# The wq gradient of seven head groups stored in five blocks each instead of one or three pieces

## The chip, the cores and the metric

The kernel runs on one core of a Trainium2 chip. The metric is the device time of one execution in microseconds (us), lower is better. Engines are named as in the profile: PE is TensorE (matmul, with its weight loads PEld), DVE is VectorE, ACT is ScalarE, POOL is GpSimd and SP is SyncE. Transfers between the device memory and the on-chip memory are issued from SP, ACT or POOL and are carried out by the core's 16 DMA engines.

## What is computed

The reference is one decode step (one token, model width 640) of a block with two parallel branches, together with the gradients of everything but the second branch's own input:

```python
xn  = layernorm(x)                                  # 1 x 640
A   = attention(xn; 32 heads of 128, K and V caches of 8192 rows each) @ wo
B   = (silu(xn @ w1) * (xn @ w3)) @ w2              # F = 1728
out = x + A + B
_out, _vjp = jax.vjp(_f, A_x, A_k_cache, A_v_cache, A_wq, A_wo, B_w1, B_w3, B_w2)
_grads = _vjp(grad_out)                             # a gradient as large as each input
```

All arrays are bf16. The two caches have 64 MB each (in units of 2^20 bytes), and so have their gradients; each is read or written once. `wq` is 640 x 4096 and its gradient `out_4` has the same shape: it is the outer product of `xn` (640 values) with the gradient of the query row (4096 values), so column block g of it belongs to the four heads of group g.

## The kernel before

**Staging.** The heads are handled one after another, h = 0 to 31. For each head one tile of K and one of V (128 partitions x 16 KB, 2 MB) is loaded into one of ten slots, transposed on PE in pieces, used for the scores, and then overwritten in place on DVE by the gradient of the same shape (`outer`, L464), which is stored from the same slot. `fifo` (L104) issues all of these on SP; SP works through its list in order. `store` (L477) issues the store of a slot and then, through `load_next` (L122), the next load into a slot that has become free, so the load waits until the slot's earlier store has landed.

**Groups.** Four heads make a group, eight groups in all (`NG`). A group has a tile `wq_g` (128 partitions x 5 blocks x 512 columns, 640 KB; block ci holds the input rows 128 ci to 128 ci + 127, one row a partition, 1 KB each) and a tile `wo_g` (640 KB). Three buffers of each kind rotate (`wpool`). `load_group` (L109) loads them, from group 3 on through POOL's queue, when the group three before is finished.

**The gradients of a group** are made one group later, spread over the next group's heads by `side_k`, `side_m` and `side_v` (L684 to L715): at its head 0 `fin_od`, `fin_pe` and `fin_wo` (the wo gradient, stored by `store_group`), at its head 1 the blocks 0, 1 and 2 of the wq gradient, at its head 2 the blocks 3 and 4. `fin_wq(g, ci)` (L524) makes one block with two DVE instructions: L527 multiplies the block by the query gradient and sums it for the input's gradient, L529 writes the block of the wq gradient over it. In the trace the five blocks of group 1 are ready at 233.5, 235.9, 240.4, 250.7 and 253.1 us. After block 4 the whole tile is stored and the loads of group g + 3 are issued behind it on POOL; these write the same buffers, so they wait for the store's landing.

**How the tile is stored.** `store_group` (L505) knows three ways. Groups 0 and 6: one POOL transfer of the whole tile (L512). Groups 1 to 5, called with `split`: partitions 0 to 4 and 5 to 125 as two POOL transfers (L508), partitions 126 and 127 through `fifo` on SP (L509, shown as L105). Group 7, at the end of the kernel: partitions 0 to 67 on SP (L514), 68 to 72 and 73 to 127 on POOL (L516). The wo gradient goes the first way for groups 0 to 6 and the third way for group 7.

**The end.** After the last head the gradients of group 7 are made all at once (L836 to L840), then the two small rows `out_0` and `out_1` are stored from SP.

**The second branch** (`mlp`, L557) runs once, ahead of head 2, and its weight gradients leave from POOL.

Of the kernel before, what the change touches and what calls it, by code (L numbers as in the profile page):

```python
# [16 lines left out]
P = 128  # L17
# [4 lines left out]
def kernel(  # L22
# [22 lines left out]
    nc = tc.nc  # L45
# [9 lines left out]
    NG = H // GH  # L55
    GW = GH * DH
# [23 lines left out]
    dwq_v = out_4.rearrange("(ci p) n -> p ci n", p=P)  # L80
# [23 lines left out]
    def fifo(out_, in_):  # L104
        nc.sync.dma_start(out_, in_)  # L105
# [3 lines left out]
    def load_group(g, eng):  # L109
        wq_g = wpool.tile([P, NC, GW], BF16, name="wq_g", tag="wq_g")  # L110
        eng.dma_start(wq_g[:], wq_v[:, :, g * GW:(g + 1) * GW])
        wo_g = wpool.tile([P, GH, D], BF16, name="wo_g", tag="wo_g")
        eng.dma_start(wo_g[:], wo_v[:, g * GH:(g + 1) * GH, :])
        grp[g] = dict(wq=wq_g, wo=wo_g)
# [387 lines left out]
        for hh in range(GH):  # L502
            out_row(G_["od_bf"][:, hh, 0:1], G_["wo"][:, hh, :])

    def store_group(g, dst, t, split=False):  # L505
        if split:
            for lo, hi in ((0, 5), (5, 126)):
                nc.gpsimd.dma_start(dst[lo:hi], t[lo:hi])  # L508
            fifo(dst[126:P], t[126:P])  # L509
            return  # L510
        if g < NG - 1:
            nc.gpsimd.dma_start(dst, t[:])  # L512
            return
        fifo(dst[0:68], t[0:68])  # L514
        for lo, hi in ((68, 73), (73, P)):
            nc.gpsimd.dma_start(dst[lo:hi], t[lo:hi])  # L516

    def fin_wo(g):
        G_ = grp[g]
        for hh in range(GH):  # L520
            nc.vector.tensor_scalar(G_["wo"][:, hh, :], g_bc[:], G_["od"][:, hh, 0:1], None, ALU.mult)
        store_group(g, dwo_v[:, g * GH:(g + 1) * GH, :], G_["wo"])

    def fin_wq(g, ci):  # L524
        G_ = grp[g]
        wq_g, dqb = G_["wq"], G_["dqb"]
        nc.vector.scalar_tensor_tensor(wq_g[:, ci, :], wq_g[:, ci, :], 1.0, dqb, ALU.mult, ALU.mult,  # L527
                                       accum_out=dxa[:, ci, g:g + 1])
        nc.vector.tensor_scalar(wq_g[:, ci, :], dqb, xn_col[:, ci:ci + 1], None, ALU.mult)  # L529
        if ci == NC - 1:  # L530
            store_group(g, dwq_v[:, :, g * GW:(g + 1) * GW], wq_g, 1 <= g <= 5)
            grp.pop(g)
            if g + 3 < NG:
                load_group(g + 3, nc.gpsimd)
# [149 lines left out]
    def side_k(h):  # L684
        g, hh = divmod(h, GH)
        if hh == 1 and g > 0:
            fin_wq(g - 1, 0)
        elif hh == 2 and g > 0:
            fin_wq(g - 1, 3)
        elif hh == 3 and g + 1 < NG:  # L690
            prep_do(g + 1, 1)

    def side_m(h):
        g, hh = divmod(h, GH)
        if hh == 0 and g > 0:
            fin_od(g - 1)
        elif hh == 1 and g > 0:
            fin_wq(g - 1, 1)
        elif hh == 2 and g > 0:
            fin_wq(g - 1, 4)  # L700
        elif hh == 3 and g + 1 < NG:
            prep_do(g + 1, 2)
            prep_do(g + 1, 3)
# [195 lines left out]
```

## Time and profile before

| | before |
|---|---|
| time, median of 3 runs | 728.27 us (727.76, 728.27, 730.0) |
| the profiled execution: its span | 728.3 us (the profile gives no other time for it) |
| bytes moved | 303.53 MB, mean 417 GB/s |
| busy share of the span: PE, DVE, ACT, POOL | 82%, 63%, 52%, 5% |
| packet time of SP's queue (q1), of POOL's (q0), as a share of 16 DMA engines | 90.4%, 8.8% |
| mean granted TensorE clock | 0.927 of full speed |

The page gives, for 40 equal slices of the span, how busy each engine and the DMA engines were; a digit is tenths. "q1 hardware_dynamic" is the queue that SP issues on and "q0 software_dynamic" the one that POOL issues on; a queue's share is the time that its packets took, out of 16 engines' span. A line of DMA issues names the tiles (destination, source), the issuing engine, how often, the size and the median time from issue to landing. In a table by stage each engine has its busy time and, in brackets, its number of instructions, followed by the granted clock, the DMA share and GB/s. The trace also holds each DMA packet (start, duration, size, queue; not which of the 16 engines took it) and, for each transfer, the times at which its semaphore rose: 16 increments where all 16 engines took part.

### The profile page before, as it was taken

How to read it: one execution, taken by the hardware profiler on the slowest of the kernel's cores; microseconds unless marked ns; L12 is line 12 of the kernel's file. 1: busy time of each engine (PE TensorE's matmuls, PEld its weight loads, DVE VectorE, ACT ScalarE, POOL GpSimd, SP SyncE). 2: the span in 40 equal slices, each digit the busy share in tenths (PEclk: the TensorE clock that was granted, in tenths of full speed). 3: DMA queues.
4: the chain of work that ended last, by engine and by line, in shares of the span. 5: the costliest groups of instructions: out<-in, count | busy, mean ns of one | idle time of the engine just before them, and what ended most of it. 6: DMA issues, size and time to landing. Idle time of an engine off the chain costs nothing.

```text
span 728.3 us, 12951 instructions
## 1 busy us (share of the span) xinstructions
PE 600.8 (82%) x5193; PEld 375.6 (52%) x5193; DVE 460.1 (63%) x811; ACT 375.7 (52%) x727; POOL 35.0 (5%) x52
## 2 busy tenths in 40 slices
PE   3989589999999999877986889878896987988840
PEld 2547456665566556544554555445563555644520
DVE  4169646677767886767556746556755665677482
ACT  3640736665666656544554546455562555645410
POOL 0010110000100000000010000000000000000000
PEclk9996799999999999999999989999998999999975
DMA  9999999999999999999999999999999999999996
GB/s 347 398 409 424 427 428 428 413 427 425 418 409 429 427 426 424 423 429 422 425 425 427 431 420 427 421 427 432 410 428 424 428 425 422 429 424 430 429 415 239
DMA packets 28358, 303.53 MB, mean 417 GB/s; under 512 B 3481, under 2 KB 5532, under 8 KB 11658
## 3 DMA queue, kind: packets, MB, share of 16 engines
q1 hardware_dynamic: 22022, 277.14, 90.4%
q0 software_dynamic: 6272, 25.56, 8.8%
q8 instruction: 41, 0.67, 0.4%
q14 instruction: 19, 0.16, 0.1%
q10 hardware_dynamic: 4, 0.00, 0.0%
HBM read 151.34 MB, written 151.34 MB: 416 GB/s over the span
## 4 chain that ended last, share of the span: by engine, by line
DMA 57%; PE 33%; DVE 5%; ACT 2%; issue 1%; SPq 0%; ACTq 0%; DVEq 0%
DMA out_dram<-kv 30%; DMA kv<-in_A_k_cache_dram 18%; PE pT L318 15%; DMA kv<-in_A_v_cache_dram 7%; PE sA L339 4%; PE X L433 3%; PE dA L339 3%; DVE kv L466 2%; PE m L356 2%; DMA wo_g<-in_A_wo_dram 2%; ACT KT L320 1%; PE gu_ps L562 1%; PE dh_ps L573 1%; DVE side L257 0%; PE pT L266 0%
## 5 line engine op out<-in xcount | busy, mean ns | idle before, releaser
L320 ACT COPY KT<-pT 128x512 f32<-128x512 f32 x512 | 287.7, 587 | 230.9 <-PE pT L318 210.3
L318 PE MATMUL pT<-ident_f,kv 128*128 128x128 f32 x2048 | 306.6, 289 | 61.6 <-DMA kv<-in_A_k_cache_dram 29.9
L318 PEld LDWEIGHTS pT<-ident_f,kv 128*128 128x128 f32 x2048 | 236.2, 148 | 155.1 <-issue 59.6
L466 DVE TENSOR_TENSOR kv<-qd,U 128x4096 bf16<-128x4096 bf16 x64 | 146.0, 2283 | 0.0
L466 DVE TENSOR_TENSOR kv<-qd,P 128x4096 bf16<-128x4096 bf16 x64 | 143.5, 2283 | 0.0
L433 PE MATMUL X<-kv,Z 128*32 128x512 bf16 x1024 | 93.5, 402 | 1.8 <-DVE Z L450 1.8
L339 PE MATMUL sA<-KT,qz 128*32 128x512 bf16 x512 | 83.9, 408 | 0.0
L339 PE MATMUL dA<-KT,qz 128*32 128x512 bf16 x512 | 83.3, 404 | 0.0
L416 DVE SCALAR_TENSOR_TENSOR U<-m,P 128x64 bf16<-128x64 f32 x32 | 7.5, 234 | 83.0 <-PE m L356 83.0
L382 DVE TENSOR_REDUCE mrow<-m 128x1 f32<-128x64 f32 x32 | 7.2, 223 | 75.1 <-PE m L356 75.0
L339 PEld LDWEIGHTS <-qz 128*32 128x32 bf16 x1024 | 29.6, 95 | 40.4 <-issue 37.7
L433 PEld LDWEIGHTS <-Z 128*32 128x32 bf16 x1024 | 32.4, 99 | 33.8 <-issue 5.7
L356 PE MATMUL m<-selc,KT 64*128 64x64 f32 x256 | 30.7, 243 | 8.6 <-ACT KT L346 8.6
L356 PEld LDWEIGHTS m<-selc,KT 64*128 64x128 f32 x256 | 21.7, 145 | 30.4 <-ACT KT L346 21.6
L376 ACT CAST qd<-pT 128x256 bf16<-128x256 f32 x32 | 11.9, 372 | 40.3 <-DVE kv L466 28.8
L389 DVE TENSOR_REDUCE negM<-m 128x1 f32<-128x128 f32 x32 | 9.3, 291 | 33.2 <-PE m L386 33.2
L527 DVE SCALAR_TENSOR_TENSOR wq_g<-wq_g,side 128x512 bf16<-128x512 bf16 x40 | 27.3, 682 | 0.0
L257 DVE SCALAR_TENSOR_TENSOR side<-wo_g,g_bc 128x640 bf16<-128x640 bf16 x32 | 26.2, 819 | 1.4 <-DMA wo_g<-in_A_wo_dram 1.1
L448 DVE SCALAR_TENSOR_TENSOR U<-m,P 128x128 bf16<-128x128 f32 x32 | 11.4, 355 | 15.8 <-PE m L446 15.8
L406 DVE RECIPROCAL rZ<-m 128x1 f32<-128x1 f32 x32 | 5.3, 166 | 24.2 <-PE m L400 24.2
L346 ACT COPY KT<-dA 64x512 f32<-64x512 f32 x32 | 18.6, 583 | 2.6 <-PE dA L339 2.6
L346 ACT COPY KT<-sA 64x512 f32<-64x512 f32 x32 | 18.6, 580 | 2.3 <-PE sA L339 2.1
(164 smaller groups left out, 377.4 us busy)
## 6 DMA issues: line engine op xcount, KB each, us to landing
out_dram<-kv SPq DMA_DIRECT2D x64, 2048.0 KB, 30.9
kv<-in_A_k_cache_dram SPq DMA_DIRECT2D x32, 2048.0 KB, 27.9
kv<-in_A_v_cache_dram SPq DMA_DIRECT2D x32, 2048.0 KB, 26.0
wq_g<-in_A_wq_dram POOLq DMA_DIRECT2D x7, 640.0 KB, 13.5
wo_g<-in_A_wo_dram POOLq DMA_DIRECT2D x7, 640.0 KB, 19.6
out_dram<-wo_g POOLq DMA_DIRECT2D x7, 640.0 KB, 15.6
kv<-in_B_w_dram SPq DMA_DIRECT2D x2, 1728.0 KB
out_dram<-kv POOLq DMA_DIRECT2D x2, 1728.0 KB, 23.2
```

The costliest lines, as they stand in the source:

```text
L257: nc.vector.scalar_tensor_tensor(junk[:], G_["wo"][:, hh, :], 1.0, g_bc[:], ALU.mult, ALU.mult, accum_out=G_["do"][:, hh:hh + 1])
L318: nc.tensor.transpose(pT[:, k * P:(k + 1) * P], W3[:, 4 * c + k, :], ident_f[:])
L320: nc.scalar.copy(KT[:].rearrange("p k w -> p (k w)"), pT[:])
L339: nc.tensor.matmul(S_[kind][q:q + QW, :], lhsT=S_["qz"][:, o:o + QW], rhs=KTb[c][:, par, :], start=(c0 == 0 and par == 0), stop=(c0 == NCH ...
L346: nc.scalar.copy(XS[0:QH].rearrange("p k w -> p (k w)"), S_.pop(kind)[0:QH, :])
L356: nc.tensor.matmul(S_["m"][:, b0:b0 + 4 * J].rearrange("p (x c k t) -> p k x c t", x=4, k=4, t=2)[:, k], lhsT=XS[0:QH, k, :], rhs=selc[0:Q ...
L376: nc.scalar.copy(qd[:].rearrange("p a d -> p (a d)"), hd[h].pop("ps_r"))
L389: nc.vector.tensor_reduce(S_["negM"][:], S_["m"][:, 2 * J:2 * J + P], AX.X, ALU.max, negate=True)
L433: nc.tensor.matmul(xg["X"][q:q + QW, :], lhsT=Z[:, o:o + QW], rhs=W[:, N4 * i:N4 * (i + 1)], start=(slot == 0 and i < 4), stop=(slot == NS ...
L448: nc.vector.scalar_tensor_tensor(S_["U2"][:], S_["V"][:, 0:J].unsqueeze(2).to_broadcast([P, J, 2]), S_["m"][:, OC + NS:OC + NS + 1], S_["P ...
L466: nc.vector.tensor_tensor(dst[:, lo * DH:hi * DH].rearrange("p (j a b) -> p j a b", a=DH // 2, b=2), vec.rearrange("p (a b) -> p a b", b=2 ...
L527: nc.vector.scalar_tensor_tensor(wq_g[:, ci, :], wq_g[:, ci, :], 1.0, dqb, ALU.mult, ALU.mult, accum_out=dxa[:, ci, g:g + 1])
```

## The change

For groups 0 to 6 each block of the wq gradient is sent from POOL directly behind the DVE instruction that makes it: five transfers of 128 partitions x 1 KB (128 KB) a group, each waiting for its own block. The whole-tile transfer of groups 0 and 6 and the three pieces of groups 1 to 5 are gone, the two partitions on SP among them. Group 7 and all wo gradients are stored as before. The loads of group g + 3 still stand on POOL's queue behind the last block.

```diff
-    def store_group(g, dst, t, split=False):
-        if split:
-            for lo, hi in ((0, 5), (5, 126)):
-                nc.gpsimd.dma_start(dst[lo:hi], t[lo:hi])
-            fifo(dst[126:P], t[126:P])
-            return
+    def store_group(g, dst, t):
         if g < NG - 1:
             nc.gpsimd.dma_start(dst, t[:])
             return
...
         nc.vector.tensor_scalar(wq_g[:, ci, :], dqb, xn_col[:, ci:ci + 1], None, ALU.mult)
+        dwq_g = dwq_v[:, :, g * GW:(g + 1) * GW]
+        if g < NG - 1:
+            nc.gpsimd.dma_start(dwq_g[:, ci, :], wq_g[:, ci, :])
         if ci == NC - 1:
-            store_group(g, dwq_v[:, :, g * GW:(g + 1) * GW], wq_g, 1 <= g <= 5)
+            if g == NG - 1:
+                store_group(g, dwq_g, wq_g)
             grp.pop(g)
             if g + 3 < NG:
                 load_group(g + 3, nc.gpsimd)
```

## The prediction

> **What bounds the kernel now.** I read the page's DMA lines first, then the list of DMA issues, the waits of GpSimd's and SyncE's queues, the busy time by stage at the end, and last the trace's own packet records (start, duration, size and queue of each DMA packet) and the landing increments of each transfer, which the page only sums.
>
> The page: the strip of DMA shares over the span, the bytes moved, and the queues.
>
> ```profile
> DMA  9999999999999999999999999999999999999996
> GB/s 347 398 409 424 427 428 428 413 427 425 418 409 429 427 426 424 423 429 422 425 425 427 431 420 427 421 427 432 410 428 424 428 425 422 429 424 430 429 415 239
> ...
> q1 hardware_dynamic: 22022, 277.14, 90.4%
> q0 software_dynamic: 6272, 25.56, 8.8%
> ```
>
> Every slice but the last is full, and the queues' packet times add up to 99.7% of what 16 engines have (90.4 + 8.8 + 0.4 + 0.1). So the time is the packet time per DMA engine plus the unevenness between engines at the end. PE (82%) and DVE (63%) wait for loads, not the other way round. GpSimd's transfers are q0, SyncE's q1.
>
> The list of DMA issues, the wq gradient's rows: how often, size, median us to landing.
>
> ```profile
> out_dram<-wq_g POOLq DMA_DIRECT2D x5, 605.0 KB, 17.0
> out_dram<-wq_g POOLq DMA_DIRECT2D x2, 640.0 KB, 13.1
> out_dram<-wq_g POOLq DMA_DIRECT2D x6, 25.0 KB, 6.7
> out_dram<-wq_g SPq DMA_DIRECT2D x5, 10.0 KB
> out_dram<-wq_g SPq DMA_DIRECT2D x1, 340.0 KB
> ```
>
> In groups 1 to 5 the tile leaves as 5, 121 and 2 partitions; in groups 0 and 6 whole. The packet records show how these spread. q0 has 55 packets of 3072 B, a size that only a share of 55 rows of 1 KB leaves (13 packets of 4 KB and one of 3 KB): five transfers on eleven engines each, 11 partitions an engine. The five partitions go to the five other engines, one each: a packet of 4 KB and one of 1 KB. A whole tile would give each engine 40 KB. So five times over, eleven engines carry 15 KB more than an even share and five carry 35 KB less.
>
> They are the same five each time. The 16 landing increments of one kv transfer lie within 2.0 us for the load issued at 5.8 us, while for the store issued at 533.0 us the first engine lands 12.9 us before the median and the last 7.5 after it. Of the last kv store (issued at 706.1), five increments come at 712.9 to 713.4 and eleven at 715.0 to 727.4; 727.4 is the last landing of all, and the span ends 0.9 us later. The first 1280 B packets of the last group's 68-partition wo piece start at 712.7 to 713.0, just as the early engines finish: that piece and the 68-partition wq piece run on four of the five. The wq piece lands on those four at 721.7, 722.5, 723.3 and 724.8.
>
> The busy time by stage (us in the stage, busy time and count of each engine, then granted clock, DMA share, GB/s):
>
> ```profile
> 690.00:695.00 5.00, 5.00 (x50) 2.86 (x47) 2.37 (x5) 3.22 (x8) 0.00 (x0) 1.00 0.97 413
> 695.00:700.00 5.00, 3.25 (x37) 1.89 (x31) 4.29 (x7) 0.93 (x2) 0.00 (x0) 1.00 0.98 419
> 700.00:705.00 5.00, 0.17 (x2) 0.08 (x1) 5.00 (x3) 0.17 (x1) 0.00 (x0) 0.50 0.93 393
> ...
> 720.00:725.00 5.00, 0.00 (x0) 0.00 (x0) 0.00 (x0) 0.00 (x0) 0.00 (x0) 0.50 0.44 153
> 725.00:728.30 3.30, 0.00 (x0) 0.00 (x0) 0.00 (x0) 0.00 (x0) 0.00 (x0) 0.50 0.04 15
> ```
>
> Before 705 us some engines already idle: (0.03 + 0.02 + 0.07) x 5 us x 16 = 9.6 us, 1.9 for each of five leaders that run out of issued stores. At the end the reverse: 0.44, then 0.04, a single engine finishing.
>
> **The change, part by part.** Durations are of the one profiled execution, whose span is 728.3 us; that is 0.03 us from the median of 728.27, so the sum needs no correction.
>
> Packet work in total. A whole tile is 160 packets of 4 KB at a median of 159 ns: 25.4 us of engine time, 1.59 per engine. The three pieces are 148 x 159 + 11 x 121 + 5 x 46 + 10 x 46 ns (SyncE's ten packets of 1 KB): 25.6 us. A block of 128 rows gives each of 16 engines 8 rows of 1 KB, two packets of 4 KB, so five blocks are again 160 packets. The nearest row, the 160 KB w2 store of 128 rows, shows such pairing: 32 packets of 5120 B. Transfers of groups 0 to 6: 35 on GpSimd instead of 12 there and 5 on SyncE, 18 more in all. Each GpSimd transfer adds one 4 B packet of 9 ns on each engine: 23 x 9 ns is 0.2 us; against that go the 81 small packets (12 and 16 B, some 10 ns) that each odd-shaped pair shows. Between -0.1 and +0.3 us; I take 0.
>
> GpSimd's issues. Five issues per group for two of 0.6 and 1.06 us; the nearest rows of 128 partitions take 0.56 to 0.88 us, so some 2 us more per group on an engine busy 5% of the span. The cover is that idle time; if it were gone, the next group's loads would start late. Each issue now also waits for its own block on DVE, and behind it in GpSimd's order stand the other blocks and the loads of group g+3. Those loads wait for the stores to land:
>
> ```profile
> POOL out_dram L508 <- DVE wq_g L529: 180.5, 5, 39.9
> POOL wq_g L111 <- DMA out_dram<-wq_g: 111.1, 4, 35.6
> ```
>
> 27.8 us each, since SyncE's two partitions lie behind kv transfers. With five GpSimd blocks the last should land in 6.7 to 13 us, and the loads start some 15 us sooner. Nobody waits: group 4's loads go out from 283.1 and their first reader on DVE comes at 332.6. Bytes moved earlier on a full engine gain nothing: 0.
>
> SyncE loses five issues of about 0.3 us and waits of 0.9 us in all for L529, beside 453 us of waiting for stores: 0.
>
> The balance is what is left. Per group, each of the five engines gets 10 packets for one and a rest: 10 x 159 - (159 + 46) = 1.39 us more, 6.9 over five groups; the two that also carried SyncE's partitions save 5 x 46 ns a group, so 5.8. Each of the eleven drops 3 x 159 + 121 = 0.60 us, 3.0 in all.
>
> The eleven: their last kv landing moves from 727.4 to 724.4.
>
> The four with the 68-partition pieces: kv done at 713.0, of which 1.9 us was idle that now disappears, so 711.2 (rounded), + 6.9 = 718.1. Then the two pieces. Before, from 713.0 to a mean landing of 723.1 is 10.1 us, the last of the four 1.7 later; from the packets at their medians it is 68 x 55 + 85 x 46 ns, 7.6 us. Below is excluded by the count of packets; above, many of the 1280 B packets took 90 to 250 ns with the other engines still at work. I take 10.1, since those engines will be at work again: 718.1 + 10.1 + 1.7 = 729.9, which is past 724.4. With 0.9 us to the end: **730.8 us**, 2.5 more than before. At 7.6 it is 728.3; if the last of the four is one that idled none of the 9.6 us, 732.7.
>
> Here the Trainium skill (DMA: Bandwidth & Descriptors, section on why a DMA increments its semaphore by 16) has a rule for the split: the largest count up to 16 that divides the rows, on consecutive engines from a round-robin cursor for GpSimd, the lowest ones for SyncE. The trace agrees in the count (121 rows on 11 engines, by 55 packets of 3072 B). The same section's exception, 16 engines with rows/16 rounded up, would leave one engine relieved instead of five; the trace's packet sizes speak against it.
>
> **The rivals.**
> *The eleven decide (faster).* The slowest of the eleven sets today's end. It sheds 3.0 us, and if the four finish their pieces before 724.4 the kernel ends at 725.3. This decides once 718.1 + pieces + 1.7 is under 724.4, so pieces under 4.6 us, or a start some 3 us earlier with pieces near 7.6. For it: two of the leaders may have idled 4 us rather than 1.9, and the 1 KB packets run at 46 ns when little else does. Against: 7.6 us of packets on engines that no longer lead.
> *The two effects cancel.* Pieces at 7.6 us on the four: 728.3, no difference.
> *Fixed cost per transfer.* 25 KB lands in 6.7 us and 605 KB in 17.0, so some 6.3 us does not scale with size. Held against the engines one after the other, 18 more transfers cost 113 us: 841. Against: the DMA share stays full while such transfers fly, and a completion packet takes 9 ns; the 6.3 us is waiting, not work. The Trainium skill (the same page, on the anatomy of one DMA and its rule to batch) puts about 2 us on each DMA and advises large transfers; by 2 us exposed, 18 would cost 36.
> *It does not do what it says*: if blocks were not spread on 16 engines, packets other than 4 KB would show. 128 rows have spread evenly in every row of this trace, so no chance is kept for it.
>
> **How the numbers follow.** A difference under 0.3% (2.2 us) is about what a measurement of this kernel cannot tell from none; the three runs span 727.76 to 730.0. Four engines late: 0.50, at 730.8. Cancelled: 0.29, at 728.3. The eleven decide: 0.19, at 725.3. Fixed cost: 0.02. The first and last are slower: 0.52. The range runs from 725.6, just inside the faster case, to 733.0, the no-idle end of the first with a little for the runs.
>
> **What would show it.** In the changed profile: no 3072 B packets, 2311 of 4 KB on q0 instead of 2251; the landings of a late kv transfer within some 12 us instead of 20; the last kv store landing at about 724.4; the 68-partition wq piece landing last, near 729.9, as the end of the chain; no 9.6 us of idle DMA before 705; GpSimd's wait at L111 roughly halved. I am wrong if the last landing is a kv store again, if the five engines still lead, or if q0's share grows by more than 0.1%.

## The result and the profile after

The changed kernel takes 731.06 us (median; 729.73 to 733.08, 22 runs) beside 728.95 us (727.72 to 731.53, 22 runs) for the kernel before: ratio 1.003, interval 1.0021 to 1.0038. It is slower by 2.1 us. The forecast was 2.5 us more. The size came out; the way to it, as the profile shows, did not.

The page of the changed kernel, DMA strip, bytes by slice and the two queues:

```profile
DMA  9999999999999999999999999999999999999994
GB/s 355 399 411 419 432 425 430 426 426 422 419 426 429 428 423 427 426 429 425 427 428 426 430 421 430 429 428 429 424 427 430 426 430 429 426 430 427 430 402 157
...
q1 hardware_dynamic: 21962, 277.09, 89.8%
q0 software_dynamic: 6160, 25.61, 8.8%
```

GpSimd's queue keeps its 8.8%: the 35 block transfers cost the DMA engines nothing that it shows. SyncE's queue has even less packet time than before (90.4%). Yet the last slice falls to 157 GB/s from 239: the work is done, and something small is left over.

The list of DMA issues of the changed kernel:

```profile
out_dram<-wq_g POOLq DMA_DIRECT2D x35, 128.0 KB, 6.8
```

GpSimd's waits (us in total, times, longest):

```profile
POOL wq_g L111 <- DMA out_dram<-wq_g: 34.4, 5, 8.1
```

A block lands in 6.8 us (median), and the loads behind the last block wait 34.4 us in all instead of 111.1. Both are as forecast. Neither is on the path that sets the end, which the landings below show.

The busy time by stage of the changed kernel (us, busy time and count of PE, PEld, DVE, ACT, POOL, then granted clock, DMA share, GB/s):

```profile
690.00:695.00 5.00, 4.70 (x45) 2.24 (x43) 3.21 (x7) 2.92 (x7) 0.00 (x0) 1.00 0.85 364
695.00:700.00 5.00, 3.30 (x26) 2.41 (x26) 4.51 (x4) 0.75 (x2) 0.00 (x0) 0.74 0.99 423
700.00:705.00 5.00, 0.00 (x0) 0.00 (x0) 5.00 (x5) 0.00 (x0) 0.00 (x0) 0.50 0.94 397
...
720.00:725.00 5.00, 0.00 (x0) 0.00 (x0) 0.00 (x0) 0.00 (x0) 0.00 (x0) 0.50 0.11 42
725.00:728.60 3.60, 0.00 (x0) 0.00 (x0) 0.00 (x0) 0.00 (x0) 0.00 (x0) 0.50 0.03 14
```

In the stretch from 720 to 725 us the DMA share is 0.11 where it was 0.44. One engine of 16 is a share of 0.06, so hardly two engines work there, and the five us cost 5 us all the same. The landing increments say who they are. These are the 16 increments of the last kv store, in us, from the trace:

```
before   712.9 713.0 713.1 713.1 713.4 715.0 716.6 719.4 720.3 721.0 722.2 722.4 723.4 724.0 724.4 727.4
after    711.6 711.7 711.7 711.8 711.9 712.6 712.7 714.2 714.8 715.0 715.8 716.4 717.0 717.4 718.4 727.3
```

Fifteen engines are done by 718.4 us, 6 us sooner than before. The sixteenth ends where the last one ended before. So fifteen engines finish sooner with the change, and one engine keeps the gain from the kernel. The 68-partition wq piece, which was to land last, lands at 720.3, 720.9, 721.2 and 722.1.

The earliest five need care. The leading engines ran out of issued work at about 693 and 701 us in both kernels (DMA shares of 0.97 and 0.93 in those stretches before, 0.85 and 0.94 after) and waited for more, so their landings in the last store no longer show how far ahead they had been. A store ahead of that point does: of the one issued at 684.0 in the changed kernel, five increments come 6.0 to 6.5 us before the median and the last 11.4 after it. Of the one issued at 682.6 in the kernel before, the first five come 5.3 to 10.4 us before it and the last 6.7 after it.

**Which engine.** A packet record doesn't name its engine, but a queue's packets follow each other closely enough to be strung into 16 sequences; two sequences can swap, so I rely on short windows only. 16 KB packets of the kv tiles take 611 ns at the median. In the changed kernel some 240 between 100 and 700 us take 640 to 700 ns, and some 200 of those lie on the sequences of one engine, which loses some 15 us over the run; the lag of the last landing behind the median one grows from 3.7 us at 247 us to 13.1 at 709. The kernel before has such an engine too: of the packets of 620 to 700 ns near each of its five split stores, most are on one engine, and in all five groups that engine carries one of the 1 KB rests that mark the 5-partition piece, and no 3072 B packet.

That makes a theory, called T1 in the expectations: one engine is slow all through the run, and in the kernel before it is, by the accident of where the pieces fall, one of the five that the split relieves. Evening out the stores gives it back 35 KB a group, and it ends last. The rivals: the number of GpSimd's transfers or their earlier issue costs time; the forecast's own account, by which the engines with the 68-partition pieces end last; or the spread counts, whichever engine is relieved. The letters T2 and T3 mean what each expectation says beside them.

### The profile page after: what moved, and what is told of

The parts are those of the page before. It is cut to its first block, busy times and chain, and to the rows that moved or that the text cites. A ratio compares the mean times of both kernels' runs of the same rounds, so it can differ in the third digit from the quotient of the medians.

```text
span 728.6 us, 12970 instructions
## 1 busy us (share of the span) xinstructions
PE 608.4 (84%) x5193; PEld 378.6 (52%) x5193; DVE 459.7 (63%) x811; ACT 376.6 (52%) x727; POOL 44.1 (6%) x75
## 4 chain that ended last, share of the span: by engine, by line
DMA 49%; PE 37%; DVE 7%; ACT 4%; issue 1%; SPq 0%; ACTq 0%; DVEq 0%
DMA out_dram<-kv 21%; PE pT L318 17%; DMA kv<-in_A_k_cache_dram 15%; DMA kv<-in_A_v_cache_dram 11%; PE sA L339 5%; PE dA L339 4%; PE X L433 4%; DVE kv L466 3%; PE m L356 2%; DMA wo_g<-in_A_wo_dram 2%; ACT KT L320 1%; ACT kv L642 1%; PE gu_ps L561 1%; DVE side L257 1%; PE dh_ps L572 1%
## 5 line engine op out<-in xcount | busy, mean ns | idle before, releaser
L433 PE MATMUL X<-kv,Z 128*32 128x512 bf16 x1024 | 102.0, 431 | 1.8 <-DVE Z L450 1.8
L339 PE MATMUL dA<-KT,qz 128*32 128x512 bf16 x512 | 85.4, 413 | 0.0
L433 PEld LDWEIGHTS <-Z 128*32 128x32 bf16 x1024 | 33.9, 104 | 38.1 <-issue 13.2
L527 POOL DMA_DIRECT2D out_dram<-wq_g x35 | 19.1, 547 | 223.1 <-DVE wq_g L524 124.3
L376 ACT CAST qd<-pT 128x256 bf16<-128x256 f32 x32 | 11.9, 373 | 38.8 <-DVE kv L466 30.4
L507 POOL DMA_DIRECT2D out_dram<-wo_g x7 | 5.3, 761 | 282.5 <-DVE qz L363 240.3
L448 DVE SCALAR_TENSOR_TENSOR U<-m,P 128x128 bf16<-128x128 f32 x32 | 11.4, 356 | 16.8 <-PE m L446 16.8
```

Of the source, the lines that this page charges most:

```text
L339: nc.tensor.matmul(S_[kind][q:q + QW, :], lhsT=S_["qz"][:, o:o + QW], rhs=KTb[c][:, par, :], start=(c0 == 0 and par == 0), stop=(c0 == NCH ...
L376: nc.scalar.copy(qd[:].rearrange("p a d -> p (a d)"), hd[h].pop("ps_r"))
L433: nc.tensor.matmul(xg["X"][q:q + QW, :], lhsT=Z[:, o:o + QW], rhs=W[:, N4 * i:N4 * (i + 1)], start=(slot == 0 and i < 4), stop=(slot == NS ...
L448: nc.vector.scalar_tensor_tensor(S_["U2"][:], S_["V"][:, 0:J].unsqueeze(2).to_broadcast([P, J, 2]), S_["m"][:, OC + NS:OC + NS + 1], S_["P ...
L527: nc.gpsimd.dma_start(dwq_g[:, ci, :], wq_g[:, ci, :])
```

## The experiments

Each is timed beside the kernel before on the same chip, and the ratio is to that. The first four ran on one chip, the next four on a second, the last three on a third.

**One whole transfer per group.** Neither blocks nor pieces: one transfer of 640 KB at the end of each group, so even stores with fewer transfers than either kernel.

```diff
-            store_group(g, dwq_v[:, :, g * GW:(g + 1) * GW], wq_g, 1 <= g <= 5)
+            store_group(g, dwq_v[:, :, g * GW:(g + 1) * GW], wq_g)
```

> The wq gradient of groups 0 to 6 leaves whole, one GpSimd transfer of 128 partitions a group after its last block: an even share on 16 engines as in the changed kernel, but at the old time and with 7 transfers instead of 35. Theory of one slow engine (one of the five engines that the old pieces relieved has slower packets, and without its relief it lands last): the same time as the changed kernel, about 731 us, 2 us over before, and the last kv store lands on one engine some 12 us behind the median. Theory of the number of transfers or of their early issue: back at the time before, about 729 us. Theory of the prediction (the 68-partition pieces of group 7 end last on engines that lost their lead): also about 731 us, but with the wq piece as the last landing.

Measured: 730.64 us (729.71 to 732.31, 12 runs), ratio 1.002 (1.0009 to 1.0031). The last kv store has fifteen increments up to 719.8 and one at 727.6, as in the changed kernel. Seven transfers instead of 35 and the late issue make no difference that shows; what the two kernels share is the even spread.

**Blocks, with the pieces inside each block.** The changed kernel, but each block of groups 1 to 5 leaves as 5 and 121 partitions, and the last two partitions on SyncE after block 4.

```diff
-        if g < NG - 1:
+        if 1 <= g <= 5:
+            for lo, hi in ((0, 5), (5, 126)):
+                nc.gpsimd.dma_start(dwq_g[lo:hi, ci, :], wq_g[lo:hi, ci, :])
+            if ci == NC - 1:
+                fifo(dwq_g[126:P], wq_g[126:P])
+        elif g < NG - 1:
```

> The changed kernel, but in groups 1 to 5 each block leaves as 5 and 121 partitions on GpSimd as it is made, and partitions 126 and 127 of the whole tile on SyncE at the end: the old spread over the engines with the new early issue, 64 GpSimd transfers of the wq gradient in groups 0 to 6 against 35. Theory of one slow engine: back at the time before, about 729 us. Theory of the number of transfers or of early issue: 731 us or more, since there are still more transfers. Theory of the prediction: about 729 us, the five engines lead again.

Measured: 732.5 us (732.09 to 732.83, 5 runs), ratio 1.0042 (1.0029 to 1.0055). It didn't restore the time. The packets say why: there is no packet of 3072 B, but 25 of 1036 B, one for each of the 25 blocks, beside 30 packets of 4 KB for each. So the 121 partitions of a block go as 8 KB on each of 15 engines and 1 KB on one. A 121-partition piece of one block isn't spread over eleven engines, as that of five blocks is. Near the split stores the slow engine shows the five 1 KB packets and ten of 4 KB: it is loaded, not relieved, and its last kv landing, 728.8, is 8.3 us after the next. So the run does not speak against T1; it was not the kernel I meant it to be. (It has 60 GpSimd transfers of these tiles, not the 64 of the expectation.) The very last landings, 729.5 and 729.6, are SyncE's 68-partition wq piece and an output row.

**One partition first.** The kernel before, with pieces of 1, 120 and 7 partitions, so that another set of engines is relieved.

```diff
-            for lo, hi in ((0, 5), (5, 126)):
+            for lo, hi in ((0, 1), (1, 121)):
                 nc.gpsimd.dma_start(dst[lo:hi], t[lo:hi])
-            fifo(dst[126:P], t[126:P])
+            fifo(dst[121:P], t[121:P])
```

> The kernel before, but the three pieces of groups 1 to 5 are partition 0, then 1 to 120 on GpSimd, and 121 to 127 on SyncE: one engine is relieved of 35 KB a group (it gets 1 partition), fifteen get 8 partitions each, seven of SyncE's engines one more. Theory of one slow engine: if it is the first of the old five, it lands some 7 us earlier than without relief while the others carry 3 us less than before, so 726 us or a little more, under the time before; if it is another of the five, about 731 us as in the changed kernel. Theory of the prediction: about 730.5 us, since the four engines of the 68-partition pieces lose most of their lead.

Measured: 734.33 us (732.38 to 736.11, 6 runs), ratio 1.0063 (1.0044 to 1.0083). The one partition leaves as five 1 KB packets on five engines, one of them the slow one, and the 120 partitions go on 15 engines with 40 KB each: 150 packets of 4 KB a group. A single engine is left out, and the slow one isn't it: its last kv landing is 730.5, 6.4 us after the next. The very last landings are later still: SyncE's 68-partition wq piece of group 7 at 732.5 and an output row at 732.7. That is the end that the forecast had described, and here it and the slow engine are 2 us apart.

**Group 7's pieces evened too.** The changed kernel without the 68, 5 and 55 partitions at the end.

```diff
-        if g < NG - 1:
-            nc.gpsimd.dma_start(dst, t[:])
-            return
-        fifo(dst[0:68], t[0:68])
-        for lo, hi in ((68, 73), (73, P)):
-            nc.gpsimd.dma_start(dst[lo:hi], t[lo:hi])
+        nc.gpsimd.dma_start(dst, t[:])
```

> The changed kernel, but group 7's wo and wq gradients leave whole on GpSimd, 40 KB of each on every engine, instead of 68 partitions on SyncE and 5 and 55 on GpSimd. Theory of one slow engine: that engine gets 80 KB at the end instead of 10, 2.8 us more, so about 734 us. Theory of the prediction: the four engines are rid of the pieces that end last, so faster than the changed kernel, 728 us or less. Theory of the number of transfers: about 731 us, no change.

Measured: 732.05 us (731.79 to 733.02, 6 runs), ratio 1.0038 (1.0026 to 1.0051). If the 68-partition pieces set the end of the changed kernel, taking them away had to help. It did not: the last kv landing is 730.0, 2.7 us later than in the changed kernel, with the next at 721.1. That fits the 2.8 us expected of 70 KB more on the slow engine, if group 7's pieces too had spared it.

**The two pieces in the other order.** This moves the relief and keeps everything else: the same two transfers by GpSimd, the same bytes, the same two partitions on SyncE.

```diff
-            for lo, hi in ((0, 5), (5, 126)):
+            for lo, hi in ((0, 121), (121, 126)):
```

> The kernel before, with GpSimd's two pieces in the other order: 121 partitions first, then 5. T1 (one of the 16 DMA engines is slower by its packets, 620 to 700 ns instead of 611, and in the kernel before it is one of the five that the 5-partition pieces relieve): if the five now fall on other engines, the slow one carries the 3072 B packets, 15 KB a group more than an even share, so its last kv landing moves from 727.3 (even stores) to 730 or later and the kernel takes 732 to 735 us. If the five stay on the same engines, the slow one still carries the 1 KB packets and the time is that of the kernel before, 729.3. T2 (the spread over engines matters, but not which engine is relieved): 729.3 in either case. T3 (the number and the early issue of GpSimd's transfers cost): 729.3 too.

Measured: 734.74 us (733.52 to 736.22, 6 runs), ratio 1.0079 (1.0061 to 1.0096). The packets of q0 are those of the kernel before, size by size (2251 of 4 KB, 55 of 3072 B, 457 of 16 B). In four of the five groups the slow engine now carries the 3072 B packet and the 4 KB ones that go with it; in the fifth the sequences swap. The last kv landing is 731.3, 5.8 us after the next, so T1's 730 or later came true. The busy time by stage:

```profile
715.00:720.00 5.00, 0.91 (x3) 0.59 (x3) 3.55 (x16) 0.00 (x0) 1.34 (x2) 0.50 0.82 290
720.00:725.00 5.00, 0.03 (x1) 0.00 (x0) 0.28 (x1) 0.00 (x0) 0.00 (x0) 0.50 0.56 189
725.00:732.50 7.50, 0.00 (x0) 0.00 (x0) 0.00 (x0) 0.00 (x0) 0.00 (x0) 0.50 0.14 50
```

A tail of 7.5 us at a share of 0.14, about two engines. With the same work and the same transfers the time goes up by 5.4 us, so it is the place of the relief that counts. That excludes both "the spread counts, whichever engine" and "the number of transfers". It does not separate the slow engine from the forecast's account, since a second engine is late too: three increments of SyncE's 68-partition wq piece come at 726.2 to 727.4 and the fourth at 731.2, and an output row lands at 731.4. The swap takes the relief from more than one engine.

**The dose: three groups split, seven, and five once more.** The only edit is the condition:

```diff
-            store_group(g, dwq_v[:, :, g * GW:(g + 1) * GW], wq_g, 1 <= g <= 5)
+            store_group(g, dwq_v[:, :, g * GW:(g + 1) * GW], wq_g, 1 <= g <= 3)
```

> The kernel before with the split only in groups 1 to 3; groups 4 and 5 leave whole. T1: the slow engine's last kv landing was 727.3 with no group split and 721.7 with five, some 1.1 us a group; the last of the eleven others 718.4 with none and 727.4 with five, 1.8 a group. With three they meet near 724, so the kernel is faster than before, 726 to 728 us. T2 (each split helps or hurts by itself, with no crossing): between none split (730.6) and five split (729.3), so 729.8.

> The kernel before with the split in groups 0 to 6 instead of 1 to 5. T1: the slow engine no longer decides, the eleven others do, and get 0.6 us (bytes) to 1.8 us a group later: last kv landing 728.6 to 731, time 730.5 to 733. T2 (more relief, more gain, in a line): 728.8.

> The kernel before, unchanged, for a second profile and to see what the comparison calls equal. T1: the slow engine's packets (620 to 700 ns) again fall on one of the five relieved engines, its last kv landing is again some 5 us before the last of all, and the last landing is again on one of the eleven. T2: which engine ends last changes from profile to profile.

Measured: three groups 727.44 us (726.77 to 729.67, 11 runs), ratio 0.9983 (0.9972 to 0.9993); seven groups (`g <= 6`) 730.88 us (728.79 to 731.55, 11 runs), ratio 1.0015 (1.0 to 1.003); five again 729.19 us (726.57 to 733.4, 12 runs), ratio 0.9995 (0.9974 to 1.0015). With none (730.64 beside 729.26) the curve has two ends up and a bottom in between, as two limits that cross would give, and a straight line can't; the intervals of none and of seven lie above that of three. The last kv store's increments, from the seventh on:

```
five, once more   714.2 719.2 720.2 720.2 720.7 721.4 723.1 723.4 723.4 724.2
three             713.5 718.8 719.2 720.7 721.1 721.9 722.2 722.3 722.6 723.7
seven             718.2 719.1 722.0 723.0 723.5 724.7 725.2 725.3 725.3 725.9
```

In each the last increment is 0.6 to 1.1 us behind the next: no engine stands alone any more in this store. With seven groups split the time came out as T1 expected, but not the end: the last kv landing was to be 728.6 to 731 on one of the eleven, and it is 725.9. What lands last there is SyncE's 68-partition wq piece, at 721.0, 721.3, 725.5 and 728.0, and an output row at 728.2. So the limit on that side is an engine with a group 7 piece, the kind of end that the forecast had, and not the kv work of the eleven. In all three kernels the slow engine carries the 1 KB rest in each split store looked at (three with three groups, five in the other two). With five groups split the last kv landing is 724.2 here and 727.4 in the profile before; this execution took 727.4 us, near the fast end of its twelve.

With three groups split this is the fastest version found. The page of it:

```profile
DMA  8999999999999999999999999999999999999996
GB/s 349 400 408 425 427 426 426 421 426 420 426 422 426 431 418 418 421 430 422 427 425 424 430 425 427 421 433 429 421 426 428 429 432 427 428 429 430 427 427 249
```

and its busy time by stage:

```profile
715.00:720.00 5.00, 0.00 (x0) 0.00 (x0) 0.00 (x0) 0.00 (x0) 0.00 (x0) 0.50 0.76 264
720.00:725.00 5.00, 0.00 (x0) 0.00 (x0) 0.00 (x0) 0.00 (x0) 0.00 (x0) 0.50 0.19 77
725.00:725.50 0.50, 0.00 (x0) 0.00 (x0) 0.00 (x0) 0.00 (x0) 0.00 (x0) 0.50 0.00 0
```

The last two slices move 427 and 249 GB/s where the changed kernel moves 402 and 157: nothing is done faster, it is spread better at the end. The last three landings are a kv store at 723.7, SyncE's 68-partition wq piece at 724.1 and an output row at 724.2, three kinds of end within 0.5 us.

**The change and the relief together.** The changed kernel, with groups 1 to 3 in the old three pieces and groups 0, 4, 5 and 6 in blocks.

```diff
-        if g < NG - 1:
+        if g < NG - 1 and not 1 <= g <= 3:
             nc.gpsimd.dma_start(dwq_g[:, ci, :], wq_g[:, ci, :])
+        if 1 <= g <= 3 and ci == NC - 1:
+            for lo, hi in ((0, 5), (5, 126)):
+                nc.gpsimd.dma_start(dwq_g[lo:hi], wq_g[lo:hi])
+            fifo(dwq_g[126:P], wq_g[126:P])
```

> The changed kernel, but groups 1 to 3 leave as in the kernel before, in 5, 121 and 2 partitions when all five blocks are made; groups 0, 4, 5 and 6 still leave block by block. T1: with the slow engine relieved three times, the block transfers cost nothing, and the time is that of the kernel before with three groups split, 727.4 us, within 0.8 of it. T3 (block transfers, 4 groups of 5 instead of 1, cost by their number): 16 more transfers than there; by the whole difference of change and kernel before, 1.8 us for 30 more on GpSimd, 1 us more: 728.4.

Measured: 727.92 us (726.21 to 730.43, 12 runs), ratio 0.9988 (0.9972 to 1.0004), where the kernel before had 728.76. Its issues of the wq rows:

```profile
out_dram<-wq_g POOLq DMA_DIRECT2D x20, 128.0 KB, 7.0
out_dram<-wq_g POOLq DMA_DIRECT2D x3, 605.0 KB, 16.9
```

Twenty block transfers in place of four whole ones, and the ratio stays within the interval of the kernel without them (0.9972 to 0.9993). The blocks cost nothing that can be seen here, but the time lies halfway between T1's 727.4 and T3's 728.4, so a cost of some tenths of a microsecond, or even T3's 1 us, is not excluded. Whole transfers without any block cost 1.4 us over the kernel before, of the change's 2.1: at least most of what the change costs comes from what it takes away.

**Two groups split.** The condition is `1 <= g <= 2`.

> The kernel before with the split in groups 1 and 2 only. T1: slow engine's last kv landing 727.3 less 2 x 1.1 to 1.4 is 724.5 to 725.1, the eleven others below 722; so the slow engine decides again and the time is 728 to 728.5, a little over the 727.4 of three groups. T2 (in a line between none, 730.6, and three, 727.4): 728.5 as well, but then the last landing is not on the slow engine.

Measured: 728.6 us (727.08 to 733.05, 12 runs), ratio 0.9999 (0.9982 to 1.0015). The time is the one expected of both theories, a little above that of three groups. But the last landing, 725.3, is only 0.7 us behind the next, so it doesn't stand alone as T1 had it, and which engine it is couldn't be followed. This point of the curve stays unexplained.

**Without SyncE's two partitions.** GpSimd sends them as a third piece. The question here is a side effect. With the split, more of the 16 KB packets of SyncE's queue take over 700 ns; what all of those take above 611 ns sums to 38.8 us of engine time in the changed kernel, 47.4 with whole transfers, 68.8 with three groups split, 89.5 and 65.6 in the two profiles of five, 90.3 with seven.

```diff
-            for lo, hi in ((0, 5), (5, 126)):
+            for lo, hi in ((0, 5), (5, 126), (126, P)):
                 nc.gpsimd.dma_start(dst[lo:hi], t[lo:hi])
-            fifo(dst[126:P], t[126:P])
```

> The kernel before, with the last two partitions sent by GpSimd as a third piece instead of by SyncE. The question is where the 16 KB packets of over 700 ns come from that appear with the split (excess over 611 ns of all such packets: 39 to 47 us of engine time with none split, 69 with three, 66 to 90 with five). If SyncE's 2-partition transfer makes them: about 45. If the 5 and 121-partition pieces do: 66 to 90. The time itself, 729 to 731 by T1, since the third piece may move the five to other engines from group to group.

Measured in one run: 98.7 us of such excess, and 732.77 us, above the 729 to 731 expected. Strung into sequences as above, the slow engine carries the 1 KB rest in groups 1 to 3 and the 3072 B packet in groups 4 and 5, so the third piece did move the relief. The last landings are SyncE's 68-partition wq piece at 729.9 and an output row at 730.1, with the last kv store at 725.9; whether the moved relief made them late, this run alone doesn't say. The long packets don't need SyncE's two-partition transfer. Whether the 5- or the 121-partition piece is, wasn't tried.

## Why the prediction was right, and where it was wrong

**The total.** Packet work was to stay the same, between -0.1 and +0.3 us, and for GpSimd's queue it did: no 3072 B packets, 2311 of 4 KB, 8.8%. SyncE's queue wasn't in the sum, and it changed: its 16 KB packets went from a mean of 618.5 to 615.3 ns. At 1024 of them an engine that is 3.2 us less, nearly all of it the packets over 700 ns (89.5 to 38.8 us over 16 engines is 3.2 each). The sum left out a gain, and the end hid it.

**GpSimd's issues, its waits, SyncE's missing issues, the earlier loads: 0.** Right as far as the runs can tell: blocks in four groups cost 0.05% of the time beside whole transfers there, within the intervals, and whole transfers in all groups are not clearly better than blocks.

**The step that failed: who is relieved.** "They are the same five each time" took the five engines that finish early for the five that the split relieves. At least one differs: the slow engine is relieved in every group and is not among the early ones in the kernel before. Nor is relief needed to be early: in the changed kernel, where nobody is relieved, five engines still lead, by 6.0 to 6.5 us in the store issued at 684.0. How many of the early five are relieved ones, and how much of their lead came from that, the runs don't settle. The reading had no way to tell the engines apart; the durations of the 16 KB packets, 620 to 700 ns on one of them, would have given it, and those were in the trace before.

**The terms that followed from it.** The early engines' kv work was to end at 718.1 instead of 713.0; it ended at 711.7, with idle time before it. Their lead on the median landing, 8.0 us on average in the store issued at 682.6 before, is still 6.3 in the one issued at 684.0 after. The pieces on them were to end at 729.9 and ended at 722.1. The eleven were to end at 724.4; all engines but the slow one ended by 718.4, where the last had ended at 727.4. Of these 9.0 us the bytes explain 3.0, and the long packets, if they were spread evenly, 3.2; the rest is open. And the 6.9 us that five engines get back was the right term, but it decided on another of the five than forecast: the slow one, at 721.7 in the kernel before as far as its sequence can be followed, moved to 727.3, by 5.6.

**The size.** That 2.5 was forecast and 2.1 measured is partly luck. A relief of 6.9 us that goes, less some slack, decides in both accounts. In the forecast the slack was the lead of the early engines less the pieces behind them; in the runs it is the room that the slow engine had before it was last. Between two profiled executions, five groups once more (727.4 us, 1.8 below its median) and the change (730.34, 0.7 below), the time differs by 2.9 us and the last kv landing by 3.1, from 724.2 to 727.3. The two profiles that the forecast is held against don't show the difference: their last kv landings are 727.4 and 727.3, the one before on an engine that is not the slow one. So the runs show what ends the changed kernel, but not what sets the end of the kernel before in each of its executions.

**Span and median.** The sum took the profiled span of 728.3 for a time 0.03 us from the median. In the later profiles, where both are known, an execution's time is 1.7 to 1.9 us above its span (730.34 for 728.6, 727.21 for 725.5). So the profile before is most likely of the run of 730.0, 1.0 us above the median of later runs, and the correction was not 0. That is why the two spans, 728.3 and 728.6, look alike while the medians differ by 2.1.

**The signs named ahead.** Right: packet sizes, q0's share, the wait at L111, which fell by more than half. Wrong: the landings (some 12 us apart; 15.7), the last kv landing, the wq piece as the last, and no idle DMA before 705: by the same reckoning (0.15 + 0.01 + 0.06) x 5 us x 16 there are 17.6 us, more than the 9.6 before. The 9.6 were not 1.9 on each of five engines either: strung into sequences, the idle time before lies on three engines, two with some 4 us and one with 1. And two of the three signs that were to show the account wrong did show: a kv store lands last, and five engines still lead.

**The rivals.** "The eleven decide" was nearest, as an engine without a 68-partition piece did set the end; but that engine was one of the five, and this was to be the faster case. The price per transfer, 36 or 113 us, is excluded.

**The skill's rules.** The forecast set aside an exception of the Trainium skill (DMA: Bandwidth & Descriptors, Why a DMA increments its semaphore by 16 and not by 1): 16 engines with a sixteenth of the partitions, rounded up. For the 605 KB pieces the 3072 B packets still speak against it. For the same 121 partitions with one block the runs show it: 15 engines with 8 KB and one with 1 KB. The same page (Latency and other measured facts) says that DMA engines 7 and 15 are usually slower than the others in traces, and offers a guess as to why. The trace agrees in kind, with one engine whose packets take 620 to 700 ns instead of 611; which number it has, and that there would be two, no run here shows.

## What to carry to other kernels

When every DMA engine is full for the whole run, the time is the last engine's, and means over 16 engines, shares and GB/s say nothing about it. Take the 16 landing increments of the last large transfer: one that stands alone by several us is an engine to be spared, and an uneven split that looks like clutter may be sparing it. Before you give work back to "the" early engines or take it from "the" late ones, find them by something that tells engines apart, such as packet durations; then vary the dose in both directions, since two limits that cross have their best point in between (here three groups of seven). Look at what lands last in each profile: here it was a kv store on the slow engine with too little relief, and a late small piece on another engine with too much or misplaced relief.

## What the runs showed of the hardware

- One of the 16 DMA engines takes 620 to 700 ns for many 16 KB packets that take 611 elsewhere, and falls 13 us behind the median engine in 709 us. It is there in the profiles of all three chips that the experiments ran on, so it is no flaw of one chip.
- The same 121 partitions are spread over eleven engines when the transfer has five blocks a partition (55 packets of 3072 B in five groups) and over sixteen when it has one (30 packets of 4 KB and one of 1036 B).
- The order of two transfers that move the same bytes, and with it the engines that they fall on, changed the time by 5.4 us, 0.8%.
- Five engines land a kv store 6.0 to 6.5 us before the median even when all stores are even (changed kernel, store issued at 684.0). The 41 instruction fetches of 16 KB (0.4% of packet time, 1 us each) lie on the other eleven, as far as their sequences can be followed, 3.7 us each, which would account for part of it; that wasn't tested.
- 16 KB packets of over 700 ns are more frequent in the runs with unevenly split stores: their time above 611 ns is 39 to 54 us in a run with even stores and 65 to 106 with split ones, summed over the engines; the cause is open.
